# Mixer's first product for the last group and half of the seventh from seven quarter products, woven into the second product of the group before

## The chip, the core and the metric

The kernel runs on one core of one Trainium2 chip. The metric is the device time of one execution in microseconds; before the change it is 366.32 us, the median of three runs (366.15 to 366.47). One more execution, timed at 365.89 us, was profiled; its span in the profile is 364.2 us. Five engines work side by side, each through its own queue in order: TensorE (PE, with its weight loads shown as PEld), VectorE (DVE), ScalarE (ACT), GpSimd (POOL) and SyncE (SP). All of them wait for each other by semaphores.

## The reference

Attention with a bias over 8 batches, 8 heads, 576 positions and head size 64, and then a mixer on its result:

```python
scores = scale * np.matmul(q, k.transpose(0, 1, 3, 2))
scores = np.where(causal, -1000000000.0, scores + np.minimum(bias, 0.0))
attn = np.exp(scores - max) ; attn = attn / (sum + 1e-09)
x = (attn @ v), heads side by side       # 8 x 576 x 512
xt = x.transpose(0, 2, 1)
h = xt @ U @ V                           # rank 32, along the positions
u = x + h.transpose(0, 2, 1)
ch = np.maximum(u @ w_ch1, 0.0) @ w_ch2  # 512 -> 2048 -> 512
return (u + ch)
```

(The softmax lines are shortened.) The change concerns the last step, `np.maximum(u @ w_ch1, 0.0) @ w_ch2`, and in it the first product, `u @ w_ch1`.

## The kernel before, in words

**Groups.** The 8 x 576 = 4608 tokens are cut into `NG` = 9 groups of 512 for the mixer, numbered 0 to 8. For each group `uT(g)` holds u transposed: 4 blocks of 128 channels by 512 tokens, bf16. The hidden layer is `hT`, 16 blocks (`NF`) of 128 hidden units by 512 tokens, bf16.

**First product.** `chanmix(g)` makes the hidden layer one block at a time: `hidden` (matmuls at L647) runs four matmuls of 512 columns, one for each block of 128 channels, into one PSUM bank (`pwork`), and ScalarE's relu (L807) writes the block of `hT`. That is 64 matmuls and 16 relus in a group. At the fourth block a DMA transpose (L814) is issued on SP that fetches u in token order (`u_sd`) for the residual.

**Second product.** For groups 1 to 8 `outputs_by_quarters` takes hT and w_ch2 each as two by two quarters and forms the product from seven quarter products in place of eight (Strassen's scheme in Winograd's form). Each quarter product (`product`, matmuls at L692, at L776 for the last of group 8) has 16 matmuls of 256 columns, in two halves of 8 with a `yield` after each. VectorE forms the sums of quarters of hT (`total`, L674: A_1, A_2, A_3, A_4, in two halves each), adds quarter products and the residual (`add`, `add_u`, L706), ScalarE copies one product (L730), and SP sends the quarters of the output (`send`, L716). The quarters of w_ch2 and their sums are made once. The sums of hT lie in `slots[3]`, `slots[4]` and `v_slots[0]`, which attention no longer needs.

**Order.** The mixer's generators stand in a list, `fill`; `step_fill` takes one step of the first of them. The main loop goes over pairs of heads, `n`: `transposes`, `scores`, `values` and, per batch, `seqmix`, which writes uT; between their steps it takes steps of `fill` at a rate set by `pace`. After the loop the rest of `fill` runs to its end. TensorE's and GpSimd's instructions keep the order in which the program issues them (`in_program_order`); those of VectorE, ScalarE and SP after the first batch are ordered by the framework's scheduler, which also puts in the semaphores. In the order that results, group 6's second product is woven with `seqmix(7)`, the last of attention; then come group 7's first product, its second, group 8's first, its second, one after the other.

**Buffers.** PSUM has 8 banks: `ps_s` has two tiles of two banks (`pscore`), `ps_w` four of one (`pwork`). `slots[0..2]` hold transposed q and k of the pairs from the second batch on, `v_slots[1]` and `v_slots[2]` v, `pTs` the exponentials, `xT` x transposed; the last batches end with them.

Of the kernel before, what the change touches and what calls it, by code (L numbers as in the profile page):

```python
# [19 lines left out]
def in_program_order(tc, first, engines):  # L20

    traced, last = tc.nc.cur_bb.bb.instructions, {}
    for ins in list(traced)[first:]:
        if ins.engine not in engines:
            continue
        prev = last.get(ins.engine)
        if prev is not None:
            tc.add_manual_dep(
                ins,
                prev.name,  # L30
                mybir.DependencyInfo(
                    mybir.DependencyClass.NoSync, mybir.DependencyReason.DATA
                ),
                reason="in_program_order",
            )
        last[ins.engine] = ins
# [3 lines left out]
def kernel(  # L40
# [31 lines left out]
    consts = ctx.enter_context(tc.tile_pool(name="consts", bufs=1))  # L72
    loads = ctx.enter_context(tc.tile_pool(name="loads", bufs=2))
    work = ctx.enter_context(tc.tile_pool(name="work", bufs=2))
    ps_s = ctx.enter_context(tc.tile_pool(name="ps_s", bufs=2, space=bass.MemoryType.PSUM))
    ps_w = ctx.enter_context(tc.tile_pool(name="ps_w", bufs=4, space=bass.MemoryType.PSUM))

    def pscore():
        return ps_s.tile([128, 1024], FP32, tag="s", name="pscore")
# [405 lines left out]
    def seqmix(b):  # L485
        x_sb = x_of.pop(b)
        up = pwork()[:, 0:128]
        for dt in range(4):
            for t in range(5):
                nc.tensor.matmul(  # L490
                    up[:, ds(dt * R, R)],
                    lhsT=x_sb[:, dt, t, :],
                    rhs=U_sb[:, t, 0:R],
                    start=(t == 0),
                    stop=(t == 4),
                    skip_group_check=True,
                )
# [36 lines left out]
        for dt in range(4):  # L534
            nc.tensor.matmul(
                banks[dt],
                lhsT=ux[ds(dt * R, R), :],
                rhs=V_sb[ds(dt * R, R), 0:512],
                start=(xT is not None),
                stop=True,  # L540
                skip_group_check=True,
            )
        pair = pair.rearrange("p (a b) -> p a b", a=2)
        for dt, src in ((slice(0, 2), pair), (2, banks[2]), (3, banks[3])):
            for lo, hi in ((0, cut), (cut, 512)):
                if lo < hi:
                    evac(dt, lo, hi, src[..., lo:hi])
            yield
        ut = pwork()[:, 0:256].rearrange("p (a b) -> p a b", a=4)
        for dt in range(4):  # L550
            if xT is None:
                nc.tensor.matmul(
                    ut[:, dt, :],
                    lhsT=x_sb[:, dt, 4, :],
                    rhs=identity[:, :64],
                    start=True,
                    stop=False,
                    skip_group_check=True,
                )
            nc.tensor.matmul(  # L560
                ut[:, dt, :],
                lhsT=ux,
                rhs=V_end[:, dt, :],
                start=(xT is not None),
                stop=True,
                skip_group_check=True,
            )
        evac(slice(0, 4), 512, S, ut)
        yield
# [112 lines left out]
    def outputs_by_quarters(g, hT, u_sd):  # L682
# [113 lines left out]
        send(o21, 1, 0)  # L796
        yield

    def chanmix(g, hT=None, done=0):
        u = uT_of.pop(g)  # L800
        if g > 0:
            hT = work.tile([128, NF, 512], BF16, tag="hT", name="hT")
            sums = weight_sums() if g == 1 else iter(())
        for nf in range(done, NF):
            f1 = pwork()
            hidden(f1, u, nf, range(4))
            nc.scalar.activation(hT[:, nf, :], f1, RELU)  # L807
            if g > 0:
                next(sums, None)
            if g > 0 and nf in (12, 14):  # L810
                first_sums(hT, nf == 12)
            if g > 0 and nf == 3:
                u_sd = work.tile([128, 4, 4, 128], BF16, tag="u_sd", name="u_sd", bufs=1)
                nc.sync.dma_start_transpose(  # L814
                    out=u_sd.rearrange("p a b c -> p (a b) c"), in_=u.rearrange("p a b -> p (a b)")
                )
            yield
        if g > 0:
            yield from outputs_by_quarters(g, hT, u_sd)
            return  # L820
        ahead = {}
        if g == 0:
            for i in range(2):
                ahead[i] = pwork()
                for _ in outputs(ahead[i], hT, i, range(8)):
                    yield
                yield
        for i in range(4):
            f2 = ahead[i] if i in ahead else pwork()
            for _ in outputs(f2, hT, i, range(8 if i in ahead else 0, NF), g == 0):  # L830
                yield
            o_sb = work.tile([128, DM], FP32, tag="o_sb", name="o_sb", bufs=3)
            if True:
                for dt in range(4):
                    nc.tensor.matmul(
                        f2[:, ds(dt * 128, 128)],
                        lhsT=u[:, dt, ds(i * 128, 128)],
                        rhs=identity,
                        start=False,
                        stop=(dt == 3),  # L840
                        skip_group_check=True,
                    )
                nc.vector.tensor_copy(o_sb, f2)
            nc.sync.dma_start(out=out_flat[ds(g * 512 + i * 128, 128), :], in_=o_sb)
            yield
# [119 lines left out]
    def load(b):  # L965
        alloc_qk(b)
        for h in range(0, H, 4 if b == 2 else H):
            load_qk(b, h, 4 if b == 2 else H)
# [36 lines left out]
    weave("S8 S9 M1 S9 M1 S9 M1 M1 S9 M1 F M1")  # L1005
    fill.append(chanmix(1))
    pace[1] = 11
    for n in range(2 * PB, NP + 2):
        b, hp = divmod(n, PB)
        if hp == 0 and b < B - 1:  # L1010
            load(b + 1)
        mixing = seqmix(b - 1) if hp == 1 and b > FT else iter(())
        if b == B:
            fill_with(3)
            for _ in range(3):
                step(mixing)
                fill_with(2)
        if n > 2 * PB and n + 1 < NP:
            for at, _ in enumerate(transposes(n + 1)):
                step_fill()  # L1020
                if at == 0:
                    step(mixing)
        if 2 * PB + 1 < n < NP:
            for at, _ in enumerate(scores(n, pT_of(n))):
                step_fill()
                if at == 1:
                    step(mixing)
        for _ in mixing:
            fill_with(1)
        if hp == 1 and b > FT:  # L1030
            fill.append(chanmix(b - 1))
            pace[1] = 12 if b < 4 else 12
        if 2 * PB < n <= NP:
            run(values(n - 1, pT_of(n - 1)))
        if hp == 0 and 2 <= b < B - 1:
            load_v(b + 1)
    pace[1] = 16
    fill.append(chanmix(NG - 1))
    while fill:
        step_fill()  # L1040
    in_program_order(tc, traced, [E.Pool, E.PE])
# [30 lines left out]
```

The softmax here doesn't subtract the row's maximum and nothing guards it: scores larger than these inputs give would overflow.

## Time and profile before

| | |
|---|---|
| time, median of 3 | 366.32 us |
| profiled run, span | 364.2 us |
| TensorE busy | 353.5 us, 3915 matmuls |
| VectorE busy | 260.7 us, 575 instructions |
| ScalarE busy | 204.2 us, 309 instructions |
| GpSimd busy | 84.8 us, 108 instructions |
| group 7's first product, its start | 307.76 us |
| group 8's second product, its start | 347.61 us |
| last DMA issue | 361.13 us |

The tail with its stages in the timeline: group 6's second product from 294.68 to 307.76, group 7's first to 321.57 and second to 333.80, group 8's first to 347.61 and second to 360.02. VectorE in the stages in between:

| stretch, us | TensorE busy | VectorE busy | ScalarE busy |
|---|---|---|---|
| 255 to 265 | 9.46 | 9.65 | 6.49 |
| 265 to 275 | 10.00 | 9.59 | 3.24 |
| 275 to 285 | 9.95 | 4.71 | 6.29 |
| 300 to 320 | 19.81 | 9.04 | 7.76 |
| 320 to 330 | 10.00 | 7.34 | 2.38 |
| 330 to 340 | 9.95 | 4.03 | 3.59 |
| 340 to 350 | 9.95 | 4.11 | 6.41 |

How to read the profile's lines: a timeline row is start and length in us, engine, source line, operation, output <- input, the shape as partitions x elements with the type, and how many; in brackets the idle time before it and what ended it. A row of several instructions is merged. A group's mean of a matmul (379 ns for 512 columns) is its length from start to result, and neighbours overlap; the pace is the distance between starts. In the chain of waits a row is start, length and what was at work. Of the matmuls a few per cent leave no record, so a count can be a little short (62 of 64).

### The profile page before, as it was taken

What the parts mean: (1) busy time and instruction counts of PE and PEld (TensorE: products, weight loads), DVE (VectorE), ACT (ScalarE), POOL (GpSimd) and SP (SyncE); (2) the same over time, 40 slices, a digit from 0 to 9 for tenths busy, and PEclk for the clock granted to TensorE, in tenths of its full rate; (3) what the DMA queues carried; (4) which work ended last, traced back from release to release, by engine and by line L of the source; (5) the groups of instructions that cost most, each with busy time, mean ns of one, the idle gap of its engine ahead of it and who ended that gap; (6) DMA issues with size and microseconds to landing.
All of it is one profiled execution on the core that took longest, in us unless ns stands there. A gap on an engine that the chain in (4) does not pass through costs nothing.

```text
span 364.2 us, 9382 instructions
## 1 busy us (share of the span) xinstructions
PE 353.5 (97%) x3915; PEld 248.6 (68%) x3959; DVE 260.7 (72%) x575; ACT 204.2 (56%) x309; POOL 84.8 (23%) x108
## 2 busy tenths in 40 slices
PE   8999999999999999999999999999999999999995
PEld 4675566665588667876688667866697577477484
DVE  8876776778789758985799569974997188075175
ACT  3875975746761677257833785358734630631620
POOL 8997462514040404040404031000000000000000
PEclk9999999999999999999999999999999999999999
DMA  7999999999997998999996999371015103303202
GB/s 108 167 201 197 170 180 107 150 139 129 113 80 97 145 136 63 79 112 129 120 92 75 150 124 72 79 137 28 11 49 133 51 18 93 83 17 104 55 29 88
DMA packets 153026, 37.41 MB, mean 103 GB/s; under 512 B 136600, under 2 KB 151352, under 8 KB 152984
## 3 DMA queue, kind: packets, MB, share of 16 engines
q0 software_dynamic: 110016, 18.50, 81.1%
q1 hardware_dynamic: 42680, 18.11, 28.6%
q8 instruction: 31, 0.51, 0.7%
q10 hardware_dynamic: 288, 0.20, 0.2%
q14 instruction: 11, 0.09, 0.1%
HBM read 37.25 MB, written 9.70 MB: 129 GB/s over the span
## 4 chain that ended last, share of the span: by engine, by line
PE 81%; DVE 10%; ACT 5%; issue 3%; DVEq 0%; ACTq 0%
PE pwork L647 30%; PE pwork L692 21%; PE pscore L401 9%; PE pwork L461 7%; PE pwork L314 4%; PE pwork L657 3%; ACT hT L807 2%; DVE uT L515 2%; DVE o_sb L706 2%; ACT pT L416 2%; DVE slot L674 2%; PE pscore L363 1%; DVE slot L337 1%; PE pscore L215 1%; PE pscore L647 1%
## 5 line engine op out<-in xcount | busy, mean ns | idle before, releaser
L647 PE MATMUL pwork<-uT,w_sb 128*128 128x512 bf16 x525 | 133.6, 379 | 2.3 <-ACT hT L807 0.5
L807 ACT ACTIVATE hT<-pwork 128x512 bf16<-128x512 f32 x140 | 84.2, 605 | 61.5 <-PE pwork L647 61.4
L416 ACT ACTIVATE pT<-pscore 128x1024 bf16<-128x1024 f32 x56 | 57.2, 1029 | 55.0 <-PE pscore L401 49.2
L647 PEld LDWEIGHTS <-w_sb 128*128 128x128 bf16 x576 | 50.7, 98 | 49.9 <-issue 0.7
L401 PE MATMUL pscore<-slot 68*128 68x320 bf16 (+1 forms) x500 | 56.0, 246 | 0.2
L401 PEld LDWEIGHTS <-slot 68*128 68x128 bf16 x564 | 41.2, 97 | 16.8 <-issue 1.3
L692 PEld LDWEIGHTS <-hT 128*128 128x128 bf16 x496 | 46.2, 98 | 7.5 <-issue 0.7
L185 POOL DMA_DIRECT2D v_slot<-in_v_dram x36 | 30.3, 856 | 78.4 <-PE pwork L461 69.4
L692 PE MATMUL pwork<-w_sb,hT 128*128 128x256 bf16 x384 | 47.5, 273 | 0.0
L346 DVE TENSOR_TENSOR pT<-pT,keep 128x512 bf16<-128x512 bf16 (+1 forms) x81 | 28.7, 354 | 21.2 <-ACT pT L416 14.8
L334 DVE COPY slot<-pwork 64x576 bf16<-64x576 bf16 x76 | 34.4, 453 | 4.7 <-PE pwork L314 3.9
L461 PEld LDWEIGHTS <-pT 128*128 128x128 bf16 x870 | 32.4, 98 | 5.3 <-issue 0.6
L461 PE MATMUL pwork<-v_slot,pT 128*128 128x65 bf16 x870 | 35.5, 193 | 0.2 <-DVE uT L515 0.2
L692 PE MATMUL pwork<-w_sum,slot 128*128 128x256 bf16 x256 | 31.5, 272 | 0.8 <-DVE o_sb L706 0.7
L471 DVE TENSOR_TENSOR x_sb<-pwork,rec 128x320 bf16<-128x320 f32 x64 | 31.2, 489 | 1.4
L427 ACT ACTIVATE pT<-pscore 128x1024 bf16<-128x1024 f32 x29 | 30.2, 1041 | 2.6 <-PE pscore L401 2.4
L674 DVE TENSOR_TENSOR slot<-hT 128x1024 bf16<-128x1024 bf16 x16 | 11.0, 688 | 24.5 <-ACT hT L807 24.3
L470 DVE RECIPROCAL rec<-pwork 128x5 f32<-128x5 f32 x64 | 12.1, 191 | 21.5 <-PE pwork L461 21.3
L692 PEld LDWEIGHTS <-slot 128*128 128x128 bf16 x256 | 24.1, 98 | 4.5 <-issue 1.6
L337 DVE COPY slot<-pwork 64x576 bf16<-64x576 bf16 x29 | 23.3, 803 | 4.9 <-PE pwork L314 3.2
L111 POOL DMA_DIRECT2D q_sd<-in_q_dram x6 | 12.6, 2107 | 45.9 <-PE pwork L314 40.6
L706 DVE TENSOR_TENSOR o_sb<-o_sb,pwork 128x512 f32<-128x512 f32 (+2 forms) x34 | 21.9, 649 | 1.0 <-PE pwork L692 0.3
(128 smaller groups left out, 414.9 us busy)
## 6 DMA issues: line engine op xcount, KB each, us to landing
out_dram<-o_sb SPq DMA_DIRECT2D x35, 256.0 KB
w_sb<-in_moe_w_ch_dram POOLq DMA_DIRECT2D x4, 1024.0 KB, 12.9
v_slot<-in_v_dram POOLq DMA_DIRECT2D x28, 128.0 KB, 6.5
q_sd<-in_q_dram POOLq DMA_DIRECT2D x5, 576.0 KB, 14.4
k_sd<-in_k_dram POOLq DMA_DIRECT2D x5, 576.0 KB, 17.9
q_sd<-in_q_dram POOLq DMA_DIRECT2D x4, 288.0 KB, 12.6
k_sd<-in_k_dram POOLq DMA_DIRECT2D x4, 288.0 KB, 11.2
q_sd<-in_q_dram POOLq DMA_DIRECT2D x4, 144.0 KB, 4.8
```

The lines of the kernel that those rows point to most:

```text
L185: nc.gpsimd.dma_start(out=vt[:rows_t, t, :, 0:D], in_=v[b, :, ds(t * 128, rows_t), :].rearrange("h p d -> p h d"),)
L334: copies(n, hh, par)(by_run[:, :, :, par, :], src)
L346: nc.vector.tensor_tensor(dst, dst, keep[:, :, 0:w].to_broadcast([128, n_tiles, w]), op=ALU.min)
L401: nc.tensor.matmul(dst, lhsT=slot[0:KA, hh, ds(S + j * 128, 128)], rhs=slot[0:KA, hh, lo:hi], start=True, stop=True,)
L416: nc.scalar.activation(pT[:, hh, 0:1024], near, EXP, scale=scale)
L427: nc.scalar.activation(pT[:, :, 1024:1536], mid.rearrange("p (a b) -> p a b", a=2), EXP, scale=scale)
L461: nc.tensor.matmul(po[:, i, :], lhsT=pT[:, hh, ds(place(j, i), 128)], rhs=vt[:, j, h, :], start=(j == 0), stop=(j == i), skip_group_check= ...
L471: nc.vector.tensor_tensor(x_sb[:, hp, :, ds(hh * D, D)], po[:, :, 0:D], rec.to_broadcast([128, 5, D]), op=ALU.mult,)
L647: nc.tensor.matmul(f1, lhsT=w1_sb[:, kt, ds(nf * 128, 128)], rhs=u[:, kt, :], start=(kt == 0), stop=(kt == 3),)
L692: nc.tensor.matmul(acc[:, i, :], lhsT=a[:, kt, ds(i * 128, 128)], rhs=b[:, kt, :], start=(i == 0 and kt == 0), stop=(kt == HF - 1), skip_g ...
L706: nc.vector.tensor_tensor(dst, a, b, op=ALU.add)
L807: nc.scalar.activation(hT[:, nf, :], f1, RELU)
```

## The change

The first product of group 8, and of half of group 7's hidden blocks, is formed as the second one is: w_ch1 (as channels x hidden) and uT are cut into two by two quarters, and seven quarter products give the four quarters of the hidden layer. A set `e` is four hidden blocks, 2e and 2e+1 of the upper half and of the lower half. Group 7 takes two sets so (blocks 0 to 3 and 8 to 11) and its other eight blocks as before (`hidden_plain`); group 8 takes four.

- **Weight sums** (`first_weight_sums`): four VectorE operations of 128x2048 elements, three of them at n = 30, 31, 32 of the main loop and one after it, held to their place on VectorE. They lie in `slots[0]`, `slots[1]`, `slots[2]` and `v_slots[2]`.
- **Token sums** (`token_sums`): four VectorE operations of 128x512 for each of the two groups, in `v_slots[1]` and in a new `xT` tile.
- **Per set** (`hidden_by_quarters`): seven products of four matmuls of 256 columns. One bank `y` gathers four products and one bank `w` two, and a `pwork` bank takes one. ScalarE copies `y` after its first, second and third product (`p1`, `U2`, `U4`, in `pTs`), VectorE adds the copies to the other products (three operations from PSUM), and the relu is ScalarE's for quarters (0,0) and (0,1); for the two lower quarters together it is ScalarE's in group 8 and VectorE's maximum in group 7. ScalarE's 24 relus of 512 from PSUM in these blocks fall away.
- **Banks**: after the main loop `ps_s` is closed, and its four banks become `ps_t`, four tiles of one bank for `y` and `w`, so that a set takes the banks that the second set before it has left.
- **Order**: the quarter products of group 7 are woven with the rest of group 6's second product and with group 7's plain blocks, those of group 8 with group 7's second product. Group 8's second product runs alone after that.
- **Second product**: unchanged, but half of its first sums are made inside `hidden_by_quarters` or right after it, and the `u_sd` transpose is issued after the hidden layer.

The diff, cut to its core:

```diff
+    ps_s_pool = tc.tile_pool(name="ps_s", bufs=2, space=bass.MemoryType.PSUM)
+    ps_s = ps_s_pool.__enter__()
...
+    def first_weight_sums():
+        for dst, a, b, op in (
+            (W_3, W11, W21, ALU.subtract),
+            (W_1, W21, W22, ALU.add),
+            (W_2, W_1, W11, ALU.subtract),
+            (W_4, W12, W_2, ALU.subtract),
+        ):
+            placed(lambda: nc.vector.tensor_tensor(dst, a, b, op=op))
+            yield
...
+    def token_sums(u, tile):
...
+        nc.vector.tensor_sub(u_3, u22, u12)
+        nc.vector.tensor_sub(u_1, u12, u11)
+        nc.vector.tensor_sub(u_2, u22, u_1)
+        nc.vector.tensor_sub(u_4, u21, u_2)
...
+        def add(e, r, c, a, b):
+            nc.vector.tensor_tensor(out(e, r, c), a, b, op=ALU.add)
+            if (r, c) == (0, 0):
+                nc.scalar.activation(out(e, r, c), out(e, r, c), RELU)
+            elif c == 0:
+                both = hT[:, ds(8 + 2 * e, 2), :]
+                if sets == 4:
+                    nc.scalar.activation(both, both, RELU)
+                else:
+                    nc.vector.tensor_scalar_max(both, both, 0.0)
...
+            if slot == 0:
...
+                product(p.y, W11, u11, e, True)
+                nc.scalar.copy(p.p1, p.y)
+                return True
+            p = parts[e]
+            if slot == 2:
+                product(p.w, W_3, u_3, e, True)
+            elif slot == 3:
+                x = two(pwork())
+                product(x, W12, u21, e, True)
+                add(e, 0, 0, p.p1, x)
+            elif slot == 4:
+                product(p.y, W_2, u_2, e, False)
+                nc.scalar.copy(p.U2, p.y)
+            elif slot == 8:
+                product(p.y, W_1, u_1, e, False)
+                nc.scalar.copy(p.U4, p.y)
+                add(e, 1, 1, p.U4, p.w)
+            elif slot == 12:
+                product(p.y, W_4, u22, e, False)
+                nc.scalar.activation(out(e, 0, 1), p.y, RELU)
+            elif slot == 13:
+                product(p.w, W22, u_4, e, False)
+                add(e, 1, 0, p.U2, p.w)
+                if sets == 4 and e in (1, 2):
+                    first_sums(hT, e == 1)
+            return True
+
+        for e in range(sets + 1):
+            for slot in range(7):
+                late = slot in (1, 5, 6)
+                if at(e - late, slot + 7 * late):
+                    yield
...
+        if NP - 2 <= n <= NP:
+            step(made_w)
...
-        if hp == 1 and b > FT:
+        if hp == 1 and FT < b < B:
             fill.append(chanmix(b - 1))
...
-    fill.append(chanmix(NG - 1))
+    ps_s_pool.__exit__(None, None, None)
+    ps_t = ctx.enter_context(tc.tile_pool(name="ps_t", bufs=4, space=bass.MemoryType.PSUM))
...
+    for g, sets, fills in ((NG - 2, 2, range(13)), (NG - 1, 4, (1, 3, 5, 7, 9, 11, 13, 16, 19, 22, 25, 25, 26, 26))):
+        u = uT_of.pop(g)
+        hT = work.tile([128, NF, 512], BF16, tag="hT", name="hT")
+        if g < NG - 1:
+            fill.append(hidden_plain(u, hT, (4, 12, 5, 13, 6, 14, 7, 15)))
+        for at, _ in enumerate(hidden_by_quarters(u, tail_sums[g], hT, sets)):
+            for _ in range(fills.count(at)):
+                step_fill()
+            if at == 3 and g < NG - 1:
+                tail_sums[NG - 1] = token_sums(
+                    uT(NG - 1), xT_again.rearrange("p a b -> p (a b)")
+                )
+        if sets < 4:
+            for one in (True, False):
+                first_sums(hT, one)
+        while fill:
+            step_fill()
+        u_sd = work.tile([128, 4, 4, 128], BF16, tag="u_sd", name="u_sd", bufs=1)
+        nc.sync.dma_start_transpose(
+            out=u_sd.rearrange("p a b c -> p (a b) c"), in_=u.rearrange("p a b -> p (a b)")
+        )
+        fill.append(outputs_by_quarters(g, hT, u_sd))
```

More of the change, by code (lines that the diff above doesn't have):

```diff
@@ L74 @@
     work = ctx.enter_context(tc.tile_pool(name="work", bufs=2))
-    ps_s = ctx.enter_context(tc.tile_pool(name="ps_s", bufs=2, space=bass.MemoryType.PSUM))
     ps_w = ctx.enter_context(tc.tile_pool(name="ps_w", bufs=4, space=bass.MemoryType.PSUM))
+    ps_s_pool = tc.tile_pool(name="ps_s", bufs=2, space=bass.MemoryType.PSUM)
+    ps_s = ps_s_pool.__enter__()
     def pscore():
@@ L797, in outputs_by_quarters, with placed, first_sum @@
         yield
+    def placed(ins_of):
+        traced = nc.cur_bb.bb.instructions
+        before = max(i for i, ins in enumerate(traced) if ins.engine == E.DVE)
+        ins_of()
+        in_program_order(tc, before, [E.DVE])
+    HW = FF // 2
+    W11, W12, W21, W22 = (
+        w1_sb[:, ds(2 * c, 2), ds(r * HW, HW)] for r in range(2) for c in range(2)
+    )
+    def first_sum(tile, free):
+        return tile.rearrange(free)[:, : 2 * HW].rearrange("p (k n) -> p k n", k=2)
+    W_3, W_1, W_4 = (first_sum(slots[i], "p a b -> p (a b)") for i in range(3))
@@ new lines, with u_quarters @@
+    W_2 = first_sum(v_slots[2], "p a b c -> p (a b c)")
+    def first_weight_sums():
[7 more added lines that the diff above has]
+            yield
+    def u_quarters(u):
+        return [u[:, ds(2 * r, 2), ds(c * 256, 256)] for c in range(2) for r in range(2)]
@@ new lines, in token_sums, with hidden_by_quarters, two, product @@
+    def token_sums(u, tile):
+        u11, u21, u12, u22 = u_quarters(u)
+        u_1, u_2, u_3, u_4 = (
+            tile[:, ds(i * 512, 512)].rearrange("p (k m) -> p k m", k=2) for i in range(4)
+        )
[3 more added lines that the diff above has]
+        nc.vector.tensor_sub(u_4, u21, u_2)
+        return u_1, u_2, u_3, u_4
+    def hidden_by_quarters(u, u_sums, hT, sets):
+        (u11, u21, _, u22), (u_1, u_2, u_3, u_4) = u_quarters(u), u_sums
+        def two(ap):
+            return ap.rearrange("p (i m) -> p i m", i=2)
+        class Part:
+            pass
+        def product(acc, w, m, e, begin):
+            for i in range(2):
+                for kt in range(2):
+                    nc.tensor.matmul(
+                        acc[:, i, :],
+                        lhsT=w[:, kt, ds((2 * e + i) * 128, 128)],
+                        rhs=m[:, kt, :],
+                        start=(begin and i == 0 and kt == 0),
+                        stop=(kt == 1),
+                        skip_group_check=True,
+                    )
+        def out(e, r, c):
+            return hT[:, ds(8 * r + 2 * e, 2), ds(c * 256, 256)]
+        def add(e, r, c, a, b):
[8 more added lines that the diff above has]
+                    nc.vector.tensor_scalar_max(both, both, 0.0)
+        parts = {}
+        def at(e, slot):
+            if not 0 <= e < sets:
+                return False
+            if slot == 0:
+                p = parts[e] = Part()
+                p.y, p.w = (
+                    two(ps_t.tile([128, 512], FP32, tag="t", name="parts")) for _ in range(2)
+                )
+                kept = pTs[e % 2].rearrange("p a b -> p (a b)").bitcast(FP32)
+                p.p1, p.U2, p.U4 = (two(kept[:, ds(i * 512, 512)]) for i in range(3))
+                product(p.y, W11, u11, e, True)
[29 more added lines that the diff above has]
+                    yield
@@ L1007 @@
     pace[1] = 11
+    made_w = first_weight_sums()
     for n in range(2 * PB, NP + 2):
@@ L1037, with hidden_plain @@
     pace[1] = 16
-    fill.append(chanmix(NG - 1))
+    ps_s_pool.__exit__(None, None, None)
+    ps_t = ctx.enter_context(tc.tile_pool(name="ps_t", bufs=4, space=bass.MemoryType.PSUM))
+    tail_sums = {}
+    tail_sums[NG - 2] = token_sums(
+        uT(NG - 2), v_slots[1].rearrange("p a b c -> p (a b c)")
+    )
+    step(made_w)
+    xT_again = work.tile([128, 4, 640], BF16, tag="xT", name="xT", bufs=1)
+    def hidden_plain(u, hT, nfs):
+        for at, nf in enumerate(nfs):
+            f1 = pwork()
+            hidden(f1, u, nf, range(4))
+            nc.scalar.activation(hT[:, nf, :], f1, RELU)
+            yield
+    for g, sets, fills in ((NG - 2, 2, range(13)), (NG - 1, 4, (1, 3, 5, 7, 9, 11, 13, 16, 19, 22, 25, 25, 26, 26))):
[9 more added lines that the diff above has]
+                    uT(NG - 1), xT_again.rearrange("p a b -> p (a b)")
+                )
+        if sets < 4:
[6 more added lines that the diff above has]
+            out=u_sd.rearrange("p a b c -> p (a b) c"), in_=u.rearrange("p a b -> p (a b)")
+        )
+        fill.append(outputs_by_quarters(g, hT, u_sd))
     while fill:
```

## The prediction, made before the change had run

> **What bounds the kernel now.** I read the page's busy shares and slices first, then the chain of waits that ended last, then TensorE's timeline of the last 60 us, and last the timelines of the engines that the change loads more.
>
> ```profile
> PE 353.5 (97%) x3915; PEld 248.6 (68%) x3959; DVE 260.7 (72%) x575; ACT 204.2 (56%) x309; POOL 84.8 (23%) x108
> PE   8999999999999999999999999999999999999995
> DVE  8876776778789758985799569974997188075175
> ```
>
> TensorE is busy in every slice. VectorE has 7s to 9s up to the 32nd slice, but holes (1, 0, 1) in the tail, where the change puts its work. The chain agrees: its last 55 us are TensorE alone.
>
> ```profile
> 321.73 12.23 PE pwork L692 x112
> ...
> 334.23 10.74 PE pwork L647 x49
> ...
> 347.77 10.49 PE pwork L692 x96
> ```
>
> TensorE's timeline gives the paces:
>
> ```profile
> 307.76 13.98 PE L647 MATMUL pwork<-uT,w_sb 128*128 128x512 bf16 x62
> 321.57 3.66 PE L692 MATMUL pwork<-w_sb,hT 128*128 128x256 bf16 x32
> ...
> 333.80 13.98 PE L647 MATMUL pwork<-uT,w_sb 128*128 128x512 bf16 x62
> 347.61 3.66 PE L692 MATMUL pwork<-w_sb,hT 128*128 128x256 bf16 x32
> ```
>
> A first product is 64 matmuls (62 records) in 321.57 - 307.76 = 13.81 us: 215.8 ns each. A second product is 112 in 12.23 us: 109.2 ns each. So 512 columns cost only 1.976 times 256 columns, and only columns saved are time saved. There is no gap to win besides.
>
> **What the Trainium skill says.** *TensorE: Matmul & The Clock Gate*, section "Wait — 56ns, not 53.3ns?": a warm matmul costs N / 2.4 GHz plus about 2.5 ns, so 109.2 and 215.8 ns; the trace agrees to 0.1 ns. *VectorE: DVE Perf Modes*, "The perf-mode tier table": tensor_tensor runs two elements a cycle on bf16 in SBUF, one with PSUM or fp32; tensor_scalar four on bf16. The trace agrees on the first part: 1024 bf16 take 0.69 us, 512 fp32 0.68; it has no bf16 tensor_scalar. *ScalarE: Activation LUTs*, "What ACT_TABLE_LOAD costs": 186 ns plus 0.833 ns per element, and neighbours overlap by about 93 ns. The trace has 605 ns for 512, and overlaps more:
>
> ```profile
> 202.00 1.02 ACT L416 ACTIVATE pT<-pscore 128x1024 bf16<-128x1024 f32 x1
> 202.92 0.59 ACT L807 ACTIVATE hT<-pwork 128x512 bf16<-128x512 f32 x1
> 203.40 1.03 ACT L416 ACTIVATE pT<-pscore 128x1024 bf16<-128x1024 f32 x1
> ```
>
> Starts are 0.92 apart after 1024 elements and 0.48 after 512: ScalarE's pace. VectorE overlaps too:
>
> ```profile
> 296.92 0.69 DVE L674 TENSOR_TENSOR hT<-hT 128x1024 bf16<-128x1024 bf16 x1
> 297.52 0.68 DVE L706 TENSOR_TENSOR o_sb<-U,u_sd 128x512 f32<-128x512 f32 x1
> 298.12 0.69 DVE L674 TENSOR_TENSOR v_slot<-hT,slot 128x1024 bf16<-128x1024 bf16 x1
> ```
>
> Starts 0.60 apart, records 0.68: I use 0.605 as its pace and 0.68 to the result.
>
> **The change part by part.**
>
> *TensorE.* A set of four hidden blocks takes 16 matmuls of 512 before (16 x 215.8 = 3.45 us), seven products of 4 matmuls of 256 after (28 x 109.2 = 3.06). Saved: 0.395 us. Six sets (two of group 7, four of group 8): 2.37 us, all on TensorE's path. The weight loads rise too, but PEld's 98 ns a load stays under 109 ns, as in L692 now.
>
> *Order.* In the built program's order the first new quarter product comes at trace time 302.5, ahead of the last 48 matmuls of group 6's second product. From there stage A (group 7's hidden layer with that rest) has 48 + 56 matmuls of 256 and 32 of 512: 18.3 us. Stage B (group 8's hidden layer with group 7's second product) has 224 of 256: 24.5 us. Then group 8's second product runs alone as now.
>
> *VectorE, stage A.* Eight token sums (128x512 bf16: 0.34 each by the bf16 rate, 2.7), one weight sum (128x2048: 1.22 by the skill's table; unmeasured here), eight output adds of group 6 (4.8), six quarter adds (fp32 with PSUM, priced as L706: 3.6), two maxima (0.4 each at four a cycle; 1.15 at one): 13.1 us in 18.3. The first 10 us are dense. TensorE's own needs in it (the u_3 sum first, W_2's at 3.9 us, W_4's at 11.7 us) come later than their results. I take nothing; dense banks could cost 0 to 0.8.
>
> *Weight sums before that.* Three of the four (1.22 each) stand earlier, two of them at about 260 to 275, where VectorE is 96% busy (9.65 and 9.59 us in two slices of 10), ahead of evacuations of pscore and pwork. TensorE could wait for a bank. But VectorE is only 4.7 busy in the next 10 us, and TensorE has other woven work queued. I take 0, bounds 0 to 1.0.
>
> *VectorE and ScalarE, stage B.* VectorE: 8 sums of group 7's second product, 12 quarter adds, 11 output adds, 4 early sums of group 8: 35 x 0.605 = 21.2 us in 24.5. ScalarE: 21 of 512 and 4 of 1024: 21 x 0.48 + 4 x 0.92 = 13.8 us. Both fit on the whole; the start doesn't. Count from stage B's first matmul. Group 8's set 2 needs the bank of set 0, freed by ScalarE's relu on its (0,1) quarter. In TensorE's order 84 matmuls stand ahead: 84 x 0.109 = 9.17 us. VectorE is free at about 0.45, and has in its order 11 operations (four of A_1 and A_2, a quarter add, two of A_3, A_4, an output add, a quarter add, A_4) before set 1's (0,0) add: 0.45 + 11 x 0.605 + 0.68 = 7.8. Behind it on ScalarE stand that quarter's relu, the copy of U2 and the relu awaited: 0.48 + 0.48 + 0.61 = 1.6, so 9.45 with the signals. TensorE waits 0.3 us, with all its queue behind it. Set 3 is alike, later: 0.1.
>
> *The end of stage B.* Set 3's last product is followed by p1 (16 matmuls, 1.75) and six of p2's before one reads the last relu: 2.40 us. The chain behind it: VectorE is in the last output add of group 7 (0.6 after), the quarter add 0.68, relu of 1024 elements 1.03: 2.4. No wait, no slack; 0 to 0.3, in the range.
>
> *DMA.* The u_sd transposes move from the fourth hidden block to the end of each stage; SP's queue keeps its order, out-sends included. Group 8's is now wanted soon: VectorE's first output add waits for it, and behind that stands A_4, needed by p3 7.0 us after stage B. So it must land in 7.0 - 0.6 - 0.7 = 5.7 us. At present the transfer after the same issue, with the same send behind it, is:
>
> ```profile
> 334.50:335.00 0.50, 0.50 (x4) 0.24 (x3) 0.43 (x1) 0.08 (x1) 0.00 (x0) 1.00 1.01 340
> ...
> 338.00:339.00 1.00, 1.00 (x7) 0.41 (x5) 0.00 (x0) 0.65 (x2) 0.00 (x0) 1.00 0.82 229
> 339.00:340.00 1.00, 1.00 (x6) 0.47 (x5) 0.00 (x0) 0.60 (x1) 0.00 (x0) 1.00 0.06 10
> ```
>
> The last two columns are the DMA share and GB/s: traffic of both is over by 339.0, 4.9 us after the issue at 334.16. It just fits; each us beyond would cost a us.
>
> *ScalarE's SBUF relu* is in no row (nearest L223, 64x576, 685 ns): 0.61 to 0.72; I take 0.61. Of the 24 relus removed none was awaited at length.
>
> *Sum.* -2.37 + 0.3 + 0.1 = -1.97 us. Span 364.2 - 2.0 = 362.2; the profiled run was timed at 365.89, the median is 366.32, so 364.35, rounded to **364.4**.
>
> **The rivals.**
>
> 1. *Forecast*: VectorE is nearly full in stage B and costs 0.2 to 1.2 of the 2.37: 364.1 to 365.1, 364.4 likeliest. For it: the paces above.
>
> 2. *No stall at all*: 366.32 - 2.37 = 363.95. For it: the 0.3 is a difference of 9.45 and 9.17. Against: three ends without slack.
>
> 3. *The gain is eaten*: an unpriced operation at its dear end (maximum, weight sums) or a transpose that lands at 7 us costs 0.7 to 1.3 us, two of them up to 2.6: 365.1 to 367.0, say 366.0. Against: 4.9 us measured, and the table's tiers.
>
> 4. *VectorE becomes the bound (slower)*: at stage B many operations read what the one before wrote, and the trace spaces such pairs 0.72 apart (318.95 to 319.67), not 0.60. If interleaving with two other engines' waits takes the overlap away everywhere, 35 x (0.69 - 0.605) = 3.0 us more: 366.32 - 1.97 + 3.0 = 367.35. It decides from a pace of 0.605 + 1.97/35 = 0.66 us. Against: the woven stretch from 296 keeps 0.60.
>
> 5. *It doesn't do what it says*: if quarter products ran at another pace than L692's, 168 of them would have to cost 14 ns more each to cancel. Same shape, same engine; inside case 3.
>
> **How the numbers follow.** Chances: forecast 0.58, no stall 0.17, eaten 0.13, VectorE-bound 0.12. A measurement of this kernel can tell about 0.2%, 0.73 us, from no change. Faster takes the first two: 0.75. Same takes case 3: 0.13. Slower takes case 4: 0.12. The range is 363.7 to 366.2: the first two cases and the nearer half of the third, 0.8 or a little more.
>
> **What would show it.** TensorE's timeline should have 256-column groups at 109 ns and waits of 0.1 to 0.5 us named after ScalarE's relu in stage B, at about its tenth and sixteenth us; stage A without waits; the second product of group 8 starting 1.5 to 2.3 us earlier than 347.61. A first output add of group 8 idle on DMA would be case 3; VectorE busy throughout stage B, with starts 0.66 apart or more, case 4. The forecast is wrong if TensorE's idle time grows by over 1.2 us.

## The result and the profile after

| | before | after |
|---|---|---|
| median, us (6 runs each, side by side) | 365.96 | 364.99 |
| ratio, 95% interval | | 0.9969 (0.9956 to 0.9983) |
| profiled execution: span, us | 364.2 | 363.2 |
| TensorE, matmuls on the page | 3915 | 4031 |
| VectorE busy, us | 260.7 | 278.0 |
| ScalarE busy, us | 204.2 | 209.6 |

The medians are over all executions; the ratios leave out those in a slower state of the chip, here one of 370.24 us after the change. By the ratio the change makes the kernel faster by 0.31%, 1.1 us of 366 (the medians differ by 0.97), where 1.97 us were forecast. The time is inside the range, 363.7 to 366.2, at its middle. On the page of the changed kernel VectorE's holes after the end of attention are filled (0 and 1 in the 35th and 38th slices before, now 6 and 9; the 1 in the 32nd is a 2) and TensorE is still full:

```profile
PE 354.2 (98%) x4031; PEld 255.9 (70%) x4031; DVE 278.0 (77%) x607; ACT 209.6 (58%) x319; POOL 84.9 (23%) x108
PE   8899999999999999999999999999999999999995
DVE  7866776779788758985699559975899279676976
```

Six sets add 168 - 96 = 72 matmuls; the weight loads show it (3959 to 4031), while the count of matmuls before lacks records.

With TensorE at 9 in all slices but the first and the last, the page can't say where one microsecond went. TensorE's timeline can: start, length, line, operation, tiles, count. These are the first quarter product of stage A, the first of stage B, the two halves of group 8's second product, and the last group of matmuls:

```profile
303.25 0.60 PE L853 MATMUL parts<-uT,w_sb 128*128 128x256 bf16 x4
...
321.53 0.60 PE L853 MATMUL parts<-uT,w_sb 128*128 128x256 bf16 x4
...
346.55 3.75 PE L693 MATMUL pwork<-w_sb,hT 128*128 128x256 bf16 x32
350.13 3.66 PE L693 MATMUL pwork<-w_sum,slot 128*128 128x256 bf16 x32
...
357.12 1.93 PE L777 MATMUL pwork<-w_sum,hT 128*128 128x256 bf16 x24
```

Stage A lasts 321.53 - 303.25 = 18.28 us, as its matmuls alone would (18.26). Stage B lasts 346.55 - 321.53 = 25.02 us where its 224 matmuls need 24.46. Group 8's second product starts 347.61 - 346.55 = 1.06 us earlier than before, not 1.5 to 2.3.

Stage B's excess stands at two places, each the first product of a new set (`parts<-uT,w_sb`):

```profile
330.26 0.60 PE L853 MATMUL parts<-xT,w_sb 128*128 128x256 bf16 x4
331.11 0.60 PE L853 MATMUL parts<-uT,w_sb 128*128 128x256 bf16 x4 [0.25 <-ACT hT L907]
...
336.35 0.60 PE L853 MATMUL parts<-xT,w_sb 128*128 128x256 bf16 x4
336.95 0.60 PE L853 MATMUL parts<-uT,w_sb 128*128 128x256 bf16 x4
```

Four matmuls take 0.44, so the second row could have started at 330.70 and the fourth at 336.79: TensorE lost 0.41 and 0.16 us. The bracket shows 0.25 and nothing, because idle time is counted from a recorded end, and a group of four is recorded as 0.60 us long where the next one can start after 0.44: the recorded end lies some 0.16 us late. Differences of starts are what to count with.

**A measure without the start of the kernel.** I call the *stretch* the time from the first matmul of `seqmix` (L490 before, L491 after) to the start of the last group of matmuls. It holds all the work that differs in the tail but the three early weight sums. The rows before, then the first row after (its last is shown above):

```profile
293.32 0.66 PE L490 MATMUL pwork<-U_sb,x_sb 128*128 128x32 bf16 x20
...
351.10 3.66 PE L692 MATMUL pwork<-w_sum,slot 128*128 128x256 bf16 x32
...
358.09 1.93 PE L776 MATMUL pwork<-w_sum,hT 128*128 128x256 bf16 x24
```

```profile
294.05 0.66 PE L491 MATMUL pwork<-U_sb,x_sb 128*128 128x32 bf16 x20
```

Before: 358.09 - 293.32 = 64.77 us. After: 357.12 - 294.05 = 63.07. The difference is -1.70 us, and it closes:

- columns saved, six sets: -2.37
- first product of set 2, stage B: +0.41
- first product of set 3: +0.16
- first half of group 8's second product, 350.13 - 346.55 = 3.58 against 351.10 - 347.61 = 3.49 before: +0.09
- sum: -1.71

Counted from the stretch's start, group 8's second product begins 54.29 - 52.50 = 1.79 us earlier, which is inside the forecast's 1.5 to 2.3.

In the profiled execution another 0.73 us was lost ahead of the stretch: its first matmul is at 294.05 instead of 293.32. The shift is already 0.71 at 29 us, where no quarter product and no weight sum has run yet, and hardly moves after that. It was 0.15 us at 14.4 us; the rest comes at a scores product (`pscore`) in the start of the kernel, whose code is the same in both; the row of before, then those of after:

```profile
15.82 0.61 PE L401 MATMUL pscore<-slot 68*128 68x128 bf16 x6
```

```profile
15.76 0.62 PE L402 MATMUL pscore<-slot 68*128 68x128 bf16 x6 [0.92 <-DMA slot<-hT]
16.65 0.60 PE L402 MATMUL pscore<-slot 68*128 68x128 bf16 x6
```

After the change, the product at 15.76 is the first with this shape; before, one had already run at 14.52, so the row at 15.82 is the second. Whether the change does this or the single execution was the first thing to ask.

### The profile page after: what moved, and what is told of

The parts are those of the page before. It is cut to its first block, busy times and chain, and to the rows that moved or that the text cites. A ratio compares the mean times of both kernels' runs of the same rounds, so it can differ in the third digit from the quotient of the medians.

```text
span 363.2 us, 9627 instructions
## 1 busy us (share of the span) xinstructions
PE 354.2 (98%) x4031; PEld 255.9 (70%) x4031; DVE 278.0 (77%) x607; ACT 209.6 (58%) x319; POOL 84.9 (23%) x108
## 4 chain that ended last, share of the span: by engine, by line
PE 77%; DVE 11%; ACT 6%; issue 3%; DMA 2%; SPq 0%; DVEq 0%; ACTq 0%
PE pwork L648 25%; PE pwork L693 20%; PE pscore L402 9%; PE pwork L462 7%; PE pwork L315 4%; PE parts L853 3%; PE pwork L658 3%; DVE slot L675 2%; ACT hT L929 2%; DVE o_sb L707 2%; DVE uT L516 2%; ACT pT L417 2%; DMA slot<-hT 2%; PE pscore L216 1%; PE pscore L648 1%
## 5 line engine op out<-in xcount | busy, mean ns | idle before, releaser
L648 PE MATMUL pwork<-uT,w_sb 128*128 128x512 bf16 x464 | 116.6, 379 | 0.7 <-ACT hT L929 0.5
L929 ACT ACTIVATE hT<-pwork 128x512 bf16<-128x512 f32 x108 | 65.1, 608 | 31.2 <-PE pwork L648 31.1
L648 PEld LDWEIGHTS <-w_sb 128*128 128x128 bf16 x480 | 41.3, 98 | 37.3 <-issue 0.7
L315 PEld LDWEIGHTS <-q_sd 72*128 72x128 bf16 x256 | 15.1, 99 | 8.5 <-DMA q_sd<-in_q_dram 0.7
## 6 DMA issues: line engine op xcount, KB each, us to landing
q_sd<-in_q_dram POOLq DMA_DIRECT2D x5, 576.0 KB, 14.4
```

Of the source, the lines that this page charges most:

```text
L315: nc.tensor.transpose(tps[hh][:, c, t2, :], src[:, 2 * hp + hh, ds(t2 * 128, 128)], identity[:TP, :TP],)
L648: nc.tensor.matmul(f1, lhsT=w1_sb[:, kt, ds(nf * 128, 128)], rhs=u[:, kt, :], start=(kt == 0), stop=(kt == 3),)
```

## The experiments

Each was timed beside the kernel before, on the same chip as it. The stretch comes from each one's profiled execution. The theory: only TensorE's columns count, less what the bank chain at the entries of sets 2 and 3 of group 8 takes. Its rivals: the late `u_sd` transpose also costs TensorE time, VectorE's load in the tail does, or the early weight sums do.

| kernel | median, us | before beside it, us | ratio, 95% interval | stretch, us |
|---|---|---|---|---|
| the change again | 364.42 | 366.43 | 0.9948 (0.9934 to 0.9962) | 63.05 |
| before again (one run) | 367.31 | 366.43 | | 64.77 |
| group 8 alone | 364.97 | 366.43 | 0.9984 (0.9951 to 1.0017) | 63.42 |
| group 7 alone | 365.51 | 366.43 | 0.9970 (0.9955 to 0.9984) | 63.99 |
| earlier fills | 363.99 | 366.15 | 0.9943 (0.9921 to 0.9966) | 62.52 |
| earlier fills, early transpose | 363.74 | 366.15 | 0.9943 (0.9929 to 0.9958) | 62.51 |
| no weaving | 370.45 | 366.15 | 1.0122 (1.0108 to 1.0135) | 69.11 |
| four sets in group 7 too | 366.36 | 366.15 | 1.0010 (0.9984 to 1.0035) | 64.75 |

### The change and the kernel before, again

Neither is edited.

> The changed kernel once more, unaltered. Between the two traces the stretch from seqmix's first matmul (L490 before, L491 after) to the last matmul is 1.70 us shorter after the change, but all of it starts 0.73 us later, because the second pair's scores waited 0.92 us for the DMA slot<-hT at 14.8 us, where neither kernel differs. Theory 1 (that wait is a chance of one execution): the wait at the start differs from 0.92 us in this trace, seqmix's first matmul starts at another time than 294.05 by 0.3 us or more, and the time is 1.3 to 2.0 us below the kernel before. Theory 2 (the changed program always pays it): the wait is 0.8 to 1.0 us again, and the time is 0.9 to 1.2 us below. In both, stage B has waits of TensorE of about 0.41 and 0.16 us at 9.2 and 15.3 us after its first matmul.

> The kernel before once more, unaltered, for a second trace of its start. Theory 1 (the start's DMA wait is chance): seqmix's first matmul starts at 293.0 to 294.2, not at 293.32 again, and the wait for slot<-hT is anything from 0 to 1 us. Theory 2 (it belongs to the changed program): 293.2 to 293.4 and no wait for slot<-hT above 0.3 us.

The stretch repeats to 0.02 us: 63.05 after 63.07, and 64.77 both times. The waits of sets 2 and 3 repeat as well (0.40 and 0.16). The start doesn't repeat. The stretch's first matmul came at 293.09 in the change (294.05 the first time) and at 294.74 in the kernel before (293.32). In the second profile of the change no product waits for that DMA at 15 us. In the second profile of before, the first wait is for `q_sd`'s DMA (0.45 us at 5.37), another at a product of 28 to 30 us is 1.27 us long instead of 0.26, its releaser unnamed, and all after it is 1.4 us later. That start, 294.74, is later than both theories forecast: they looked at the wait for `slot<-hT` alone, and other waits vary too. Over the ten profiles of this case the stretch began between 293.05 and 294.74. So the 0.73 us belongs to one execution and not to the change. The second comparison, 364.42 against 366.43, gives -2.0 us and a ratio whose interval overlaps the first one's.

### Group 8 alone

```diff
-    for g, sets, fills in ((NG - 2, 2, range(13)), (NG - 1, 4, (1, 3, 5, ...))):
...
+    fill.append(chanmix(NG - 2))
...
+    g, sets, fills = NG - 1, 4, (1, 3, 5, 7, 9, 11, 13, 16, 19, 22, 25, 25, 26, 26)
```

> Only group 8's first product from quarter products (four sets); group 7's hidden layer is made as before, and the rest of group 6's second product runs ahead of it. Saved on TensorE: 4 x 0.395 = 1.58 us. Group 7's first sums of one half are then made during its hidden layer, so VectorE enters stage B with four operations fewer (2.4 us). If VectorE's queue at the start of stage B causes the 0.41 us wait, that wait is gone here, the later one of 0.1 to 0.2 us stays, and the kernel is 1.3 to 1.6 us below the kernel before, from seqmix to the last matmul 1.4 to 1.5 us. If the wait comes from ScalarE's own load or from the banks alone, it stays at 0.4 us and only 1.0 us is won.

Measured: 63.42, that is -1.35 us, a little short of the expectation. Four sets save 1.58. The entry of set 3 still waits 0.16 (336.68 where 336.52 was possible), and 0.08 is lost in the first half of the second product: -1.34. The 0.41 at set 2 is gone:

```profile
330.41 0.60 PE L853 MATMUL parts<-xT,w_sb 128*128 128x256 bf16 x4
330.85 0.60 PE L853 MATMUL parts<-uT,w_sb 128*128 128x256 bf16 x4
```

TensorE's queue ahead of it is the same as in the change. What differs is VectorE's: without quarters in group 7, half of group 7's first sums run before stage B. VectorE's timeline of this kernel:

```profile
319.05 0.69 DVE L675 TENSOR_TENSOR slot<-hT 128x1024 bf16<-128x1024 bf16 x1 [8.82 <-ACT hT L929]
...
320.99 0.68 DVE L675 TENSOR_TENSOR v_slot<-hT,slot 128x1024 bf16<-128x1024 bf16 x1
```

These four are out of the way when stage B starts at 321.68. VectorE's add for set 1's (0,0) quarter then starts at 327.99, 6.31 us into stage B, where it started at 7.22 in the change (328.75 - 321.53), and ScalarE runs the same operations behind it. So the set 2 wait comes from VectorE's queue at the entry. The wait at set 3 does not: it stays at 0.16. The times don't settle the gain of this kernel: the interval includes 1.

### Group 7 alone

```diff
-    for g, sets, fills in ((NG - 2, 2, range(13)), (NG - 1, 4, (1, 3, 5, ...))):
+    for g, sets, fills in ((NG - 2, 2, range(13)),):
...
+    fill.append(chanmix(NG - 1))
```

> Only half of group 7's hidden blocks from quarter products (two sets, woven as in the change); group 8 as before. Saved on TensorE: 2 x 0.395 = 0.79 us, with no wait in stage A: 0.7 to 0.8 us from seqmix to the last matmul. If the changed program's start costs 0.7 us always, the whole gain is 0.0 to 0.1 us; if that was chance, 0.6 to 0.9 us.

Measured: 63.99, -0.78 us; two sets save 0.79. Group 7's part, its early weight sums and stage A's dense VectorE queue cost TensorE nothing. The two parts alone give -0.78 and -1.35, together -2.13; both at once gave -1.70 to -1.72. The 0.41 that is missing is the wait that only both together have.

### Earlier fills

The second product's blocks of group 7 are woven one step earlier into group 8's quarter products, and spread to the end:

```diff
-(NG - 1, 4, (1, 3, 5, 7, 9, 11, 13, 16, 19, 22, 25, 25, 26, 26))
+(NG - 1, 4, (0, 2, 4, 6, 8, 10, 12, 14, 17, 20, 23, 25, 26, 27))
```

> The changed kernel with one line altered: in stage B the steps of group 7's second product stand after quarter products 0, 2, 4 ... instead of 1, 3, 5 ..., so that 8 matmuls more (0.87 us) stand ahead of set 2's and set 3's first products. If the two waits (0.41 and 0.16 us) are just a bank that comes 0.2 to 0.4 us too late, they go: the stretch from seqmix's first matmul to the last matmul falls from 63.05 to 62.4 to 62.6 us (64.77 - 2.37 = 62.40 is the count of columns alone), and the kernel is 0.4 to 0.6 us faster than the change. If VectorE were short of time all through stage B, the waits would only move: 63.0 us again.

Measured: 62.52, 0.55 us less than the change, with no instruction added or taken away. Counted along TensorE's timeline, 92 matmuls stand between the starts of sets 0 and 2 instead of 84, which gives ScalarE's relu 0.87 us more. The bank is free before TensorE wants it; ScalarE, then TensorE:

```profile
330.01 0.58 ACT L907 ACTIVATE hT<-parts 128x512 bf16<-128x512 f32 x1
```

```profile
331.08 0.60 PE L853 MATMUL parts<-uT,w_sb 128*128 128x256 bf16 x4
```

Set 0's relu ends at 330.59. The entry of set 3 and the start of the second product have no gap either. The columns alone would give 64.77 - 2.37 = 62.40; 0.10 of the rest is a gap in front of a product at 325.85. In time this kernel is at 0.9943 of before. The change was at 0.9948 and 0.9969, measured on other occasions, and the intervals overlap: the 0.55 us between the two is shown by the profiles, not by the times.

### Earlier fills, and the transpose early

As above, and group 8's `u_sd` lies in `v_slots[1]`, free by then, so that its transpose is issued ahead of the hidden layer:

```diff
+        else:
+            u_sd = v_slots[1].rearrange("p a b c -> p (a b c)")[:, :2048].rearrange(
+                "p (a b c) -> p a b c", a=4, b=4
+            )
+            nc.sync.dma_start_transpose(...)
```

> Like even_fills, and group 8's u_sd lies in v_slots[1], which is free after stage A, so that its transpose is issued at the start of stage B and not at its end. VectorE's first output add of the last second product then doesn't wait for it (0.86 us in one trace of the change, 0.39 in the other). If the 5.7 us that the prediction allowed are right, no matmul waits for that chain and the stretch is that of even_fills within 0.1 us; if the late transpose reaches TensorE, it is 0.2 to 0.5 us shorter.

In the change the transpose is late. SyncE's queue and VectorE's first output add of group 8 in the profile after:

```profile
346.53 3.22 SPq L1196 DMA_TRANSPOSE u_sd<-uT  x1
```

```profile
351.89 0.69 DVE L707 TENSOR_TENSOR o_sb<-U,u_sd 128x512 f32<-128x512 f32 x1 [0.86 <-issue]
```

From issue to use it took 5.36 us, and VectorE idled 0.86. With earlier fills alone it idles 1.14 and the add runs at 350.83; with the early transpose the add runs at 348.59 without a wait, and the stretch is 62.51 against 62.52. So the transpose was late for VectorE and cost TensorE nothing.

### No weaving

All of the preceding group's second product runs ahead of the quarter products, and group 7's plain blocks behind them. The work is the same:

```diff
+        while fill:
+            step_fill()
         for at, _ in enumerate(hidden_by_quarters(u, tail_sums[g], hT, sets)):
-            for _ in range(fills.count(at)):
-                step_fill()
```

> The same instructions, but not woven: before each stage's quarter products the rest of the second product of the group before runs to its end, and group 7's plain blocks come after its quarter products. TensorE's columns are the same. A set then has 3.06 us on TensorE, but ScalarE's part is 5 x 0.48 + 0.92 = 3.3 us, and each product into the bank y must wait until the copy of the one before is made (0.2 + 0.6 us). Theory 1 (the other product's matmuls hide that chain): waits of 0.3 to 0.9 us all along the quarter products, 3 to 7 us together, the stretch 65.5 to 69.5 us and the kernel 1 to 4 us slower than before. Theory 2 (the count of columns decides): 62.4 to 63.1 us as in the change.

Measured: 69.11 us, 6.0 more than the change and 6.6 more than with earlier fills. In time it is 1.2% slower than before, 4.3 us by the medians, a little over the forecast of 1 to 4. Group 8's 112 quarter matmuls need 12.23 us and take 352.26 - 335.35 = 16.91; the other 2.0 us are lost around group 7's sets. Three of the waits, all in the last set of group 8:

```profile
348.15 0.60 PE L853 MATMUL parts<-uT,slot 128*128 128x256 bf16 x4 [0.41 <-ACT pT L903]
349.35 0.60 PE L853 MATMUL parts<-xT,w_sb 128*128 128x256 bf16 x4 [0.60 <-DVE hT L866]
...
351.11 0.60 PE L853 MATMUL parts<-uT,slot 128*128 128x256 bf16 x4 [0.73 <-ACT pT L903]
```

The quarter products alone can't keep TensorE busy: each set passes a bank from TensorE to ScalarE and back several times.

### Four sets in group 7 too

Group 7 takes four sets, has no plain blocks, and its sums and relus are made as group 8's are. Group 8's steps stand as with earlier fills, so this kernel is compared with that one (62.52), not with the change. The diff is shown against the change, without the line for group 8:

```diff
-(NG - 2, 2, range(13))
+(NG - 2, 4, (0,3,6,9,12,15,18))
...
-fill.append(hidden_plain(u, hT, (4, 12, 5, 13, 6, 14, 7, 15)))
+fill.append(hidden_plain(u, hT, ()))
```

> Group 7's hidden layer wholly from quarter products too (four sets, its lower relus on ScalarE), woven with the rest of group 6's second product; group 8 as in the change. TensorE saves 8 x 0.395 = 3.16 us. VectorE in stage A then has 8 token sums (2.7), a weight sum (1.2), 8 output adds (4.8), 12 quarter adds (7.3) and 4 early sums (2.4): 18.4 us against TensorE's 160 x 0.109 = 17.5. If VectorE decides, TensorE waits 1 to 3 us in stage A, most of it in the later sets, where no second product is left to weave, and the stretch is 62.6 to 64.6 us: no better than the change although it has 0.79 us of matmuls less. If the count of columns decides, it is 61.6 to 62.2 us.

Measured: 64.75, over what was expected and no better than the kernel before. Two more sets save 0.79 us of columns. But stage A now has 160 matmuls of 256 (17.47 us) and lasts 323.19 - 302.69 = 20.50: 3.03 us of waits. 62.52 - 0.79 + 3.03 = 64.76. The waits all stand after the last of group 6's second product, which ends near 315:

```profile
316.32 0.60 PE L853 MATMUL parts<-uT,w_sb 128*128 128x256 bf16 x4 [0.37 <-ACT hT L907]
...
319.08 0.60 PE L853 MATMUL parts<-uT,slot 128*128 128x256 bf16 x4 [0.41 <-ACT pT L903]
320.27 0.60 PE L853 MATMUL parts<-v_slot,w_sb 128*128 128x256 bf16 x4 [0.60 <-DVE hT L866]
...
322.04 0.60 PE L853 MATMUL parts<-uT,slot 128*128 128x256 bf16 x4 [0.73 <-ACT pT L903]
```

By starts, the gaps ahead of these four are 0.53, 0.58, 0.75 and 0.89 us, and another of 0.28 follows: 3.03. The last three brackets are those of the unwoven kernel's last set. The stretch is near the one forecast for a VectorE that decides, but VectorE's load is not what decides here: from 302.7 to 315.0, where it is busy 11.90 of 12.30 us, TensorE loses nothing, and in the 8.2 us after that, where all the waits stand, it is busy 6.36, as ScalarE is.

Stage A has only 48 matmuls of a second product, six steps, to weave in. For two sets the plain blocks supply the rest; without them the gain of columns is given back almost four times. Another spread of the six steps over the four sets was not tried.

## Why the prediction was right, and where it was off

**The gain.** 2.37 us from columns: group 7 alone gave -0.78 for 0.79, and 62.52 is within 0.12 us of all six sets with no wait. Rival 5 (it doesn't do what it says) falls with that. Rival 2 (no stall at all) is refuted for the change, which loses 0.66 us, and nearly true of the kernel with earlier fills.

**The reading of VectorE's row.** "7s to 9s up to the 32nd slice" was loose: the slices ahead of it hold 5s, 6s and a 4 too, and the 32nd is itself a hole, in which attention still runs. No term of the sum rests on it.

**Stage A.** Forecast 18.3 us and no wait; measured 18.28 and none.

**Weight sums.** Taken at 0, bounds 0 to 1.0. The shift between the two first profiles was 0.71 at 29 us and 0.73 at 293, and group 7 alone, which has these sums, misses its columns by 0.01: they cost nothing.

**The wait at set 2.** Its place, its chain and its sign were right; the size was 0.41 for 0.3. The forecast's chain, VectorE and then ScalarE:

```profile
328.75 0.68 DVE L866 TENSOR_TENSOR hT<-pT,pwork 128x512 bf16<-128x512 f32 x1
```

```profile
329.46 0.63 ACT L868 ACTIVATE hT<-hT 128x512 bf16<-128x512 bf16 x1 [2.13 <-DVE hT L866]
330.00 0.57 ACT L900 COPY pT<-parts 128x512 f32<-128x512 f32 x1
330.46 0.60 ACT L907 ACTIVATE hT<-parts 128x512 bf16<-128x512 f32 x1
```

VectorE began its eleven operations at 322.12, that is 0.59 us into stage B and not 0.45, and kept a pace of (328.75 - 322.12) / 11 = 0.603. Its result was there at 7.90 (forecast 7.8). ScalarE's three took 331.06 - 329.46 = 1.60 (forecast 1.57), and TensorE went on 0.05 later, at 9.58 instead of 9.45. TensorE was ready at 9.17, as forecast. The term mis-sized is VectorE's entry: 0.14 of it. Its last operations of stage A, ahead of the eleven:

```profile
320.87 0.69 DVE L866 TENSOR_TENSOR hT<-pT,parts 128x512 bf16<-128x512 f32 x1 [1.26 <-PE parts L853]
321.59 0.43 DVE L874 TENSOR_SCALAR hT<-hT 128x1024 bf16<-128x1024 bf16 x1
322.12 1.29 DVE L675 TENSOR_TENSOR slot<-hT 128x1024 bf16<-128x1024 bf16 x2
```

VectorE had no backlog there: it idled 1.26 us for stage A's last quarter product, and from the start of the add to the start of the first of the eleven it was 1.25 us, with the maximum, which reads the add's result, in between.

**The wait at set 3.** 0.16 for 0.1, but not by the chain that was forecast. "Set 3 is alike" was wrong in its mechanism: VectorE's queue had run dry by then, and the group 8 kernel, with VectorE's queue shorter at the entry, waits the same 0.16. VectorE, then ScalarE:

```profile
334.81 0.69 DVE L866 TENSOR_TENSOR hT<-pT,pwork 128x512 bf16<-128x512 f32 x1 [0.27 <-PE pwork L853]
```

```profile
335.30 0.59 ACT L900 COPY pT<-parts 128x512 f32<-128x512 f32 x1 [1.48 <-PE parts L853]
335.78 0.63 ACT L868 ACTIVATE hT<-hT 128x512 bf16<-128x512 bf16 x1
336.31 0.59 ACT L907 ACTIVATE hT<-parts 128x512 bf16<-128x512 f32 x1
```

Both engines had waited for TensorE's products. The relu that frees the bank stands third in ScalarE's order and ends at 336.90; TensorE could have used the bank at 336.79. That the size came near the forecast is luck. This chain is read from the timeline; no run changes ScalarE's order alone.

**The end of stage B.** "No wait, no slack; 0 to 0.3" was taken at 0 and measured 0.09. Together the three terms are 0.26 us over the forecast, which is the difference between -1.97 and the -1.71 of the stretch.

**VectorE as the bound (rival 4).** It needed a pace of 0.66 or more in stage B. In its densest part starts stay 0.60 apart:

```profile
341.02 0.69 DVE L675 TENSOR_TENSOR slot<-slot,hT 128x1024 bf16<-128x1024 bf16 x1
341.62 0.68 DVE L707 TENSOR_TENSOR o_sb<-o_sb,pwork 128x512 f32<-128x512 f32 x1
342.22 0.68 DVE L866 TENSOR_TENSOR hT<-pT,parts 128x512 bf16<-128x512 f32 x1
```

And between 330 and 337 us it stands idle five times, for up to 1.06 us. The interleaving seems to keep the pace at 0.60, since an operation that reads its predecessor's result rarely stands right behind it here; where one does, the starts are 0.73 apart (349.01 and 349.74).

**Rival 3 (the gain is eaten).** The unpriced operations came out at their cheap ends: the maximum of 1024 bf16 elements took 0.43 us, which agrees with four elements a cycle in *VectorE: DVE Perf Modes* of the Trainium skill, "The perf-mode tier table", and the SBUF relu of 512 took 0.63 (estimate 0.61). The transpose came closest. It was estimated to land after 4.9 us by the DMA traffic of before, with a limit of 5.7; it took 5.36 the first time and 4.9 (345.55 to 350.44) the second. It stayed under the limit, and the run with an early transpose shows that nothing was lost. So the sign that the forecast named for this rival, an idle first output add of group 8, did appear (0.86 us) without the loss: the limit decides, not the idle time.

**What the forecast didn't have** is the variation of the start of the kernel between executions. Measured as a time, the gain was 1.0 us in one comparison of medians and 2.0 in the other; in the stretch it was 1.70 and 1.72. The forecast of 1.97 lies close to the second comparison by chance of the sample: its own terms were 0.26 us too favourable. Why the first comparison's medians differ by only 1.0 is shown for its profiled execution alone; of the other executions the profile says nothing. The forecast time, 364.4, looks better than the forecast gain for another reason: it started from 366.32, the median of three runs, and six runs gave 365.96. The gain in that comparison was 1.0 us short, and 0.36 of it doesn't show in the time.

## What to carry to other kernels

Where an engine is full, a change of its work is worth the work that it saves, less the waits that its own new dependencies make at the entries; find these by laying each engine's queue side by side up to the first reuse of a bank. Interleaving is part of the price: the same instructions unwoven were 1.2% slower than before, one step of weaving earlier gave back 0.55 us, and more of the cheaper products than there was foreign work to weave gave all back. Judge a change of under 1% by a stretch between two marks in the trace that encloses it: that repeated to 0.02 us here, where the gain in the whole time came out as 1.0 us once and as 2.0 the second time.

## What was unexpected

- The first matmul of the last stretch came between 293.05 and 294.74 us over ten profiles, and in the four profiles compared the shift came from waits in the first 30 us: for DMAs (0.92 and 0.45 us) and one whose releaser the profile does not name (up to 1.27). What stood behind kept the shift.
- A `u_sd` transpose of 128 x 2048 bf16 took 4.9 to 5.4 us from issue to use in three profiles (both of the change, and earlier fills), with output sends beside it; its own record on SyncE's queue is 3.1 to 3.3 us there.
- The recorded wait of a matmul was 0.16 us shorter than the gap between starts, and a gap of that size was not recorded at all.
